# Interleaving GpSimd's weight loads with the scaling of v, ten more idle matmuls, and one group of scores behind the first MLP columns

## The chip, the core and the metric

The kernel runs on one core of one Trainium2 chip. The metric is the device time of one execution in microseconds (us). Before the change it is 312.73 us, the median of three runs (312.11 to 313.31). Five engines work side by side: TensorE (PE) multiplies matrices into PSUM banks; VectorE (DVE) and ScalarE (ACT) move PSUM results to SBUF and do elementwise work; GpSimd (POOL) works from SBUF to SBUF; SyncE (SP) only issues transfers. SP, ACT and POOL each have a DMA queue of their own, called q1, q10 and q0 in the profile.

## What is computed

The first half is a retention layer over 8 batches, 8 heads, 576 positions and a head width of 64. The second half is an MLP over the 4608 tokens that result.

```python
scores = scale * q @ k.T                       # per batch and head
gamma = 1.0 - 2.0 ** (-5.0 - arange(H))
Dmat = where(rel >= 0, gamma ** rel, 0.0)      # rel = row - column
x = ((scores * Dmat) @ v)                      # -> [4608 tokens, 512]
h = x @ w_in                                   # 512 -> 2048
out = (h * cos(h)) @ w_out                     # 2048 -> 512
```

## The kernel before, in words

**Retention.** A batch is cut into chunks of 128 positions (r = 0 to 3, and a short r = 4 with 64). The decay is split into a factor on q (table UP or UPN) and one on v (table WV), so that only a triangle mask is left for the scores. For each chunk PE does four things. `scores` multiplies k and q; its two results (one per head of a pair) are masked by two DVE operations of 128x512 (`mask`, L538). `sums_q` multiplies q by the state that the earlier chunks left in the SBUF tile `sb`, and `sums_v` adds the masked scores times v; the sum is copied into the tile `xt` (L595). `state` adds this chunk's k times v to the PSUM tile `st`, and two ACT copies (L616) take that to the next `sb`. `state` needs k of the chunk and the scaled v (tile `vb`) that POOL makes in `vmul` (L359). A scores group that is marked "later" has its second mask put behind the next MLP column group's multiplication on DVE.

**MLP.** The tokens go in 9 blocks of 512. `mlp1` makes one of 16 column groups (dt): four matmuls into a PSUM bank, the cosine on ACT (L644), the product on DVE (L647) into the tile `gt`. `mlp2` makes 128 rows of output from four parts of four matmuls each. There are four PSUM banks (`mm`) that `bank()` hands out in turn, so a column group has to wait until DVE has emptied the bank that was handed out four groups earlier. Block 1 is begun with the first 320 of its 512 tokens (SP1), since its last tokens belong to batch 2.

**Weights.** w_in comes in four pieces: columns for dt 0-1, 2-3, 4-7 and 8-15 (`WI`, L26). The first is loaded by SP as float32 into the space of q (`w_in_first`, L320) and turned to bf16 by one DVE operation of 128x1024 (`w_in_cast`, L330). The other three are loaded by POOL (`w_in_load`, L338), which converts on the way; so are the four pieces of w_out (L345).

**Order.** Everything is written out by hand in `emit` (L714 to L863); each engine does its instructions in that order and waits on semaphores. SP issues batch 0's k and q, v of chunks 0 to 3, the first piece of w_in (after POOL's casts of q have freed the space), and v of chunk 4. POOL casts k and q, scales v of chunk 0, issues w_in pieces 1 and 2, scales v of chunks 1 to 3, issues piece 3 and then w_out (L732 to L742). PE transposes k and q (`turn0`, `back0`), makes batch 0's scores (`scores0`, one group of 8 matmuls for each pair of heads, both results masked on DVE), then states and sums for chunks 1 and 2 (L765 to L770), then block 0's columns. DVE gets `w_in_cast` (L763) after the last masks and before the copies of the sums of chunks 1 and 2. `spin(n, bank)` (L498) issues n matmuls of 128x512 on a tile of zeros; nobody reads the result. In front of block 1 stand `turn_k(1, 2)` (a transposition of k, copied by ACT at L415), `rest(1, 1)` (sums and state of chunk 1), `scores(1, 2)` and one idle matmul (L816 to L819).

Of the kernel before, what the change touches and what calls it, by code (L numbers as in the profile page):

```python
# [48 lines left out]
class Sched:  # L49
# [36 lines left out]
    def done(self, eng, inst, reads, writes):  # L86
        self.count[eng] += 1
        inst.then_inc(self.sem[eng], 1)
        clock = {s: v for s, (v, _) in self.seen[eng].items()}
        t = Tok(eng, eng, self.count[eng], clock)  # L90
        self.record(t, reads, writes)
        return t
# [32 lines left out]
class _Kernel:  # L125
# [588 lines left out]
    def emit(self):  # L714
# [15 lines left out]
        self.w_in_first()  # L730
        self.load("v", 0, NCH - 1)
        self.vmul("pool", 0, 0)  # L732
        self.w_in_load(1)
        self.w_in_load(2)
        for r in range(1, NCH - 1):
            self.vmul("pool", 0, r)
        self.w_in_load(3)
        wo = []
        for i in range(NWO):
            wo.append(self.w_out_load(i))  # L740
# [3 lines left out]
        po, st = (self.PO, self.bPO), (self.ST, self.bST)  # L744
        mm, sc = list(zip(self.MM, self.bMM)), list(zip(self.SC, self.bSC))
        sc = [sc, [po, mm[3]]]
        self.spin(7, st)
        for c in range(NP):
            self.turn0("k", c, mm[0], "act" if c else "dve")
            if c:  # L750
                self.back0(c - 1, st)
            else:
                self.spin(1, mm[3])
            self.turn0("q", c, mm[1 + c % 2], "dve")
            if c < 2:
                self.spin(1, mm[3])
            if c:
                self.scores0(c - 1, sc[(c - 1) % 2])
        self.back0(3, st)
        self.state(0, 0)()  # L760
        self.scores0(3, sc[1])
        outs = [mm[0], mm[1], mm[2], sc[0][0]]
        self.w_in_cast()  # L763
        self.spin(3, mm[0])
        for r in (1, 2):  # L765
            done = self.state(0, r)
            self.sums_q(0, r, outs[r])
            done()
            for i in range(0 if r == 1 else 2, r + 1):
                self.sums_v(0, i, outs[i], "dve" if i else "act")()  # L770
        self.n_mm = 3
        self.vmul("pool", 0, NCH - 1)
        for r in range(NCH):
# [41 lines left out]
        self.flush()  # L815
        self.turn_k(1, 2, self.bank())  # L816
        self.rest(1, 1, self.bank())
        self.scores(1, 2)
        self.spin(1)  # L819

        for dt in range(16):
            self.mlp1(1, dt, 0, SP1)
            if dt in (7, 13):
                self.scores(1, 2 + dt // 6, True)
            if dt in (3, 9):
                self.turn_k(1, 3 + dt // 6)
            if dt in (5, 11):
                self.rest(1, 2 + dt // 6)
# [63 lines left out]
```

## Time and profile before

| what | number |
|---|---|
| median of three runs | 312.73 us (312.11 to 313.31) |
| the profiled execution | 312.78 us, of which the span of the profile is 311.0 us |
| PE busy | 303.1 us, 97% of the span |
| DVE, ACT, POOL busy | 178.3, 161.2, 106.5 us |
| mean granted TensorE clock | 0.995 |
| PE busy from 0 to 15.5 us, from 15.5 to 24 us | 11.38 of 15.5, 7.92 of 8.5 us |
| PE busy from 80 us to the end | 228.5 of 231 us |

All times in the views are counted from the start of the span. A row of a timeline gives the start, the length, the engine, the line, the operation, the tiles (output <- inputs), the number of instructions merged into it and, in brackets, the engine's idle time just before with what ended it. A row of the chain of work gives start, length, engine and line; the chain is followed back from the last instruction, so whatever stands in it set the end. In tables of stretches the columns are the stretch, its length, the busy time of each engine with its count of instructions, the granted PE clock (1.00 is full), the busy share of the DMA engines, and GB/s.

### The profile page before, as it was taken

What the parts mean: (1) busy time and instruction counts of PE and PEld (TensorE: products, weight loads), DVE (VectorE), ACT (ScalarE), POOL (GpSimd) and SP (SyncE); (2) the same over time, 40 slices, a digit from 0 to 9 for tenths busy, and PEclk for the clock granted to TensorE, in tenths of its full rate; (3) what the DMA queues carried; (4) which work ended last, traced back from release to release, by engine and by line L of the source; (5) the groups of instructions that cost most, each with busy time, mean ns of one, the idle gap of its engine ahead of it and who ended that gap; (6) DMA issues with size and microseconds to landing.
All of it is one profiled execution on the core that took longest, in us unless ns stands there. A gap on an engine that the chain in (4) does not pass through costs nothing.

```text
span 311.0 us, 6450 instructions
## 1 busy us (share of the span) xinstructions
PE 303.1 (97%) x2538; PEld 159.0 (51%) x2538; DVE 178.3 (57%) x318; ACT 161.2 (52%) x288; POOL 106.5 (34%) x129
## 2 busy tenths in 40 slices
PE   6799999999999999999999999999999999999996
PEld 3574455666644455445544554455445554444444
DVE  5857644887548842785368554855487448405800
ACT  8658407875447433753277236723573347316711
POOL 4881046645565636354646554510000000000000
PEclk9979999999999999999999999999999999999999
DMA  7999999999999999999999998950101010120022
GB/s 230 252 198 208 208 216 247 250 229 182 249 222 179 233 208 228 181 229 200 251 195 221 237 222 195 191 136 34 36 0 70 34 36 0 40 98 0 1 76 95
DMA packets 138319, 49.12 MB, mean 158 GB/s; under 512 B 127921, under 2 KB 132273, under 8 KB 138289
## 3 DMA queue, kind: packets, MB, share of 16 engines
q1 hardware_dynamic: 128880, 34.88, 61.8%
q10 hardware_dynamic: 5184, 9.31, 8.9%
q0 software_dynamic: 4224, 4.52, 8.7%
q8 instruction: 20, 0.33, 0.5%
q14 instruction: 11, 0.08, 0.1%
HBM read 36.70 MB, written 9.44 MB: 148 GB/s over the span
## 4 chain that ended last, share of the span: by engine, by line
PE 92%; SPq 3%; DMA 2%; ACT 1%; DVE 0%; issue 0%; ACTq 0%
PE mm L511 62%; PE mm L513 20%; PE po L511 5%; PE sc L511 3%; DMA qn<-in_moe_w_in_dram 2%; SPq L288 2%; SPq L296 1%; PE st L511 1%; ACT osb L681 1%; PE po L513 0%; ACT kqt L415 0%; DVE win L330 0%; DVE xt L595 0%; ACT xt L595 0%; ACT sb L616 0%
## 5 line engine op out<-in xcount | busy, mean ns | idle before, releaser
L647 DVE TENSOR_TENSOR gt<-mm,cb 128x512 bf16<-128x512 f32 (+3 forms) x164 | 101.6, 626 | 61.2 <-ACT cb L644 58.6
L511 PE MATMUL mm<-xt,win 128*128 128x512 bf16 (+3 forms) x492 | 119.1, 353 | 0.5 <-DVE xt L595 0.4
L644 ACT ACTIVATE cb<-mm,c_pih 128x512 bf16<-128x512 f32 (+3 forms) x164 | 102.8, 636 | 31.1 <-PE mm L513 30.7
L511 PE MATMUL mm<-wout,gt 128*128 128x512 bf16 (+1 forms) x450 | 117.4, 373 | 0.0
L511 PEld LDWEIGHTS mm<-xt,win 128*128 128x128 bf16 x492 | 46.4, 98 | 48.8 <-DVE xt L595 1.0
L511 PEld LDWEIGHTS mm<-wout,gt 128*128 128x128 bf16 x450 | 41.0, 98 | 42.2 <-DVE gt L647 0.2
L513 PE MATMUL mm<-xt,win 128*128 128x512 bf16 (+3 forms) x164 | 57.9, 353 | 0.0
L513 PE MATMUL mm<-wout,gt 128*128 128x512 bf16 (+1 forms) x142 | 53.6, 378 | 0.0
L681 ACT ACTIVATE osb<-mm 128x512 f32<-128x512 f32 x35 | 20.9, 597 | 62.5 <-PE mm L513 62.5
L359 POOL TENSOR_TENSOR vb<-vn,wv 128x512 bf16<-128x512 f32 (+1 forms) x40 | 41.6, 1042 | 11.3 <-DMA vn<-in_v_dram 10.1
L595 DVE CAST xt<-po 128x512 bf16<-128x512 f32 (+1 forms) x34 | 21.3, 627 | 40.5 <-PE po L513 40.5
L370 POOL CAST kqb<-kn 128x512 bf16<-128x512 f32 (+1 forms) x35 | 21.3, 610 | 66.7 <-DMA kn<-in_k_dram 61.7
L616 ACT ACTIVATE sb<-st 64x256 bf16<-64x256 f32 x64 | 24.2, 377 | 35.7 <-PE st L513 34.7
L359 POOL TENSOR_TENSOR kqb<-qn,upn 128x512 bf16<-128x512 f32 (+1 forms) x30 | 31.3, 1042 | 14.5 <-DMA qn<-in_q_dram 13.6
L538 DVE TENSOR_TENSOR rt<-sc,mk 128x512 bf16<-128x512 f32 (+1 forms) x52 | 29.1, 597 | 6.5 <-PE sc L513 6.5
L513 PEld LDWEIGHTS mm<-xt,win 128*128 128x128 bf16 x164 | 16.0, 98 | 15.4
L513 PEld LDWEIGHTS mm<-wout,gt 128*128 128x128 bf16 x142 | 13.9, 98 | 16.5
L511 PE MATMUL po<-rt,vb 128*64 128x128 bf16 (+1 forms) x245 | 13.6, 220 | 0.0
L538 DVE TENSOR_TENSOR rt<-mm,mk 128x512 bf16<-128x512 f32 x20 | 12.8, 681 | 0.0
L511 PEld LDWEIGHTS po<-rt,vb 128*64 128x64 bf16 (+1 forms) x245 | 8.3, 108 | 5.5 <-DVE rt L538 2.1
L511 PE MATMUL sc<-kqt 64*128 64x128 bf16 (+1 forms) x196 | 10.3, 213 | 0.8 <-ACT kqt L415 0.8
L511 PE MATMUL st<-vb,kqb 128*64 128x64 bf16 x224 | 9.5, 198 | 1.5 <-POOL vb L359 0.8
(126 smaller groups left out, 166.5 us busy)
## 6 DMA issues: line engine op xcount, KB each, us to landing
out_dram<-osb ACTq DMA_DIRECT2D x35, 256.0 KB, 3.4
vn<-in_v_dram SPq DMA_DIRECT2D x32, 256.0 KB, 5.1
kn<-in_k_dram SPq DMA_DIRECT2D x28, 256.0 KB, 4.1
qn<-in_q_dram SPq DMA_DIRECT2D x24, 256.0 KB, 4.6
wout<-in_moe_w_out_dram POOLq DMA_DIRECT2D x4, 512.0 KB, 15.7
kn<-in_k_dram SPq DMA_DIRECT2D x4, 288.0 KB, 5.1
qn<-in_q_dram SPq DMA_DIRECT2D x4, 288.0 KB, 5.4
vn<-in_v_dram SPq DMA_DIRECT2D x8, 128.0 KB, 4.3
```

The lines of the kernel that those rows point to most:

```text
L288: return self.s.dma(eng, f"{x}n{r}", lambda e: e.dma_start(dst, src), writes=[self.bST32[x][r]], after=after)
L296: self.s.dma("sp", f"{x}0_{c}", lambda e: e.dma_start(dst, src), writes=[self.bN0[x][c]])
L359: self.s.op(eng, lambda e: e.tensor_tensor(bass.AP(t, o, [[pitch, ck], [D_, H_], [1, D_]]), self.staged(x, r, [[D_, H_], [1, D_]]), bass.A ...
L370: fn = (lambda e: e.activation(o, f, AF.Copy)) if eng == "act" else (lambda e: e.tensor_copy(o, f))
L511: self.nc.tensor.matmul(o, a, b, **kw)
L513: return s.done("pe", self.nc.tensor.matmul(o, a, b, **kw), reads, writes)
L538: self.s.op("dve", lambda e: e.tensor_tensor(bass.AP(self.RT[k][hp], 0, p3), bass.AP(sc[0], 0, p3), bass.AP(self.MK, 0, [[CH, ck], [0, NP] ...
L595: fn = (lambda e: e.activation(o, f, AF.Copy)) if eng == "act" else (lambda e: e.tensor_copy(o, f))
L616: s.op("act", lambda e: e.activation(bass.AP(self.SB[r % 3], 64 * hp * 512 + 64 * hp, [[512, 64], [128, NP], [1, D_]]), bass.AP(self.ST, 6 ...
L644: s.op("act", lambda e: e.activation(co, mo, AF.Sin, bias=self.C_PIH.ap(), scale=1.0), reads=[bm, self.bC], writes=[bcb])
L647: s.op("dve", lambda e: e.tensor_tensor(bass.AP(g, dt * TB + o, [[16 * TB, 128], [1, n]]), mo, co, ALU.mult), reads=[bm, bcb], writes=bg[o ...
L681: s.op("act", lambda e: e.activation(o.ap(), m.ap(), AF.Copy), reads=[bm], writes=[bo])
```

## The change

Three edits in `emit`, and no other.

```diff
         self.vmul("pool", 0, 0)
-        self.w_in_load(1)
-        self.w_in_load(2)
         for r in range(1, NCH - 1):
             self.vmul("pool", 0, r)
-        self.w_in_load(3)
+            self.w_in_load(r)
...
                 self.scores0(c - 1, sc[(c - 1) % 2])
+        self.spin(1, mm[0])
         self.back0(3, st)
+        self.spin(3, mm[0])
         self.state(0, 0)()
         self.scores0(3, sc[1])
         outs = [mm[0], mm[1], mm[2], sc[0][0]]
         self.w_in_cast()
-        self.spin(3, mm[0])
+        self.spin(2, mm[0])
         for r in (1, 2):
             done = self.state(0, r)
             self.sums_q(0, r, outs[r])
             done()
+            if r == 1:
+                self.spin(4, mm[0])
             for i in range(0 if r == 1 else 2, r + 1):
                 self.sums_v(0, i, outs[i], "dve" if i else "act")()
+        self.spin(2, po)
...
         self.turn_k(1, 2, self.bank())
         self.rest(1, 1, self.bank())
-        self.scores(1, 2)
-        self.spin(1)
+        self.spin(2)
 
         for dt in range(16):
             self.mlp1(1, dt, 0, SP1)
-            if dt in (7, 13):
+            if dt in (0, 7, 13):
                 self.scores(1, 2 + dt // 6, True)
```

First, POOL's order for batch 0 becomes v0, v1, w_in piece 1, v2, piece 2, v3, piece 3, where it was v0, pieces 1 and 2, v1, v2, v3, piece 3. Second, idle matmuls are added at four places of batch 0 and one is taken away at a fifth (1 + 3 - 1 + 4 + 2 = 9 more), and the single one in front of block 1 becomes two, which makes ten in all. Third, the scores of batch 1's chunk 2 go from the place in front of block 1 to the place behind its first column group, and their second mask goes behind the second column group's product on DVE.

## The prediction

> **What bounds the kernel now.** I read the page's chain of work first. It ends in a row of PE shares:
>
> ```profile
> PE 92%; SPq 3%; DMA 2%; ACT 1%; DVE 0%; issue 0%; ACTq 0%
> ```
>
> From 24 us on PE never rests for long, so a change there counts only if it takes work or a wait from PE. The 8% that are not PE lie at the start. So the second view is the chain in order of time, from 11 to 20 us (start, length, what):
>
> ```profile
> 11.47 6.26 DMA qn<-in_moe_w_in_dram
> 17.73 0.02 issue
> 17.75 0.93 DVE win L330
> 18.68 0.60 DVE xt L595
> 19.29 0.05 issue
> 19.33 0.50 PE mm L511 x3
> ```
>
> The reader is to see that the first column group of block 0 (PE at 19.33) waits for the copy of chunk 1's sums, that this copy stands on DVE behind the cast of w_in's first piece, and that the cast waits for that piece's transfer, landed at 17.73. From landing to PE it is 19.33 - 17.73 = 1.60 us. Neither PE nor POOL sets this: in PE's timeline the sums of chunk 1 were issued by 17.3.
>
> The third view is the table of stretches of 1 us (PE, PEld, DVE, ACT, POOL busy, clock, DMA share, GB/s):
>
> ```profile
> 14.00:15.00 1.00, 0.81 (x5) 0.19 (x3) 1.00 (x3) 0.52 (x2) 0.98 (x2) 1.00 0.84 193
> 15.00:16.00 1.00, 0.39 (x9) 0.35 (x10) 0.49 (x1) 0.00 (x0) 1.00 (x2) 0.72 1.03 229
> 16.00:17.00 1.00, 1.00 (x16) 0.80 (x16) 0.00 (x0) 0.76 (x2) 1.00 (x2) 0.50 1.09 214
> 17.00:18.00 1.00, 1.00 (x23) 0.94 (x20) 0.25 (x1) 0.77 (x2) 1.00 (x2) 0.50 1.33 185
> 18.00:19.00 1.00, 0.89 (x12) 0.45 (x9) 1.00 (x2) 0.59 (x2) 1.00 (x3) 0.58 1.24 196
> ```
>
> The granted clock falls to 0.50 for (0.28 + 0.50 + 0.50 + 0.42) x 2 = 3.4 us, from about 15.4 to 18.8, after a stretch in which PE was busy half the time. It is full again at 19.33, where PE comes onto the chain. So in this execution the half clock costs nothing, and idle matmuls that prevent it bring nothing by themselves.
>
> **Edit 1, POOL's order.** The queues' view shows what shares the DMA engines. From 14.75 to 15.25 only q1 (SP's) moves; from 15.25 to 17.5 q0 (POOL's) moves too (packets, MB, share):
>
> ```profile
> q1 hardware_dynamic: 188, 0.17, 115.0%
> ```
>
> ```profile
> q0 software_dynamic: 357, 0.18, 64.0%
> q1 hardware_dynamic: 279, 0.27, 50.0%
> ```
>
> q1 alone runs at 0.17 MB / 0.5 us, about 343 GB/s; beside q0 at 0.27 / 2.25, 120 GB/s. Piece 1, which POOL issues at 12.71, is what slows the first piece of w_in: q0's first packets come at 15.25 to 15.35, some 2.6 us after the issue began. In the new order v1 comes first. Its transfer was issued at 5.54 and takes 7.3, landing at 12.85; `vmul` takes 1.04; so POOL issues piece 1 at about 13.95 instead of 12.71, and q0's packets come at about 13.95 + 2.6 = 16.6. Until then the first piece has the engines alone. Its last 0.27 MB at 343 GB/s take 0.8 us, so it would end at 16.05 instead of 17.5 (gain 1.4, the one bound). But the engines are not in step: v3's transfer, just ahead on q1, still has a tail in the stretch from 14.75, and an engine that starts the piece at 15.1 with 32 packets of 1 KB, at the 50 ns that 343 GB/s over 16 engines gives, ends at 16.75. The other bound is no gain, if q0's packets come as early as before. I take landing at 16.9, a gain of **0.8**, near the late engine.
>
> Is PE ready then? State of chunk 1 waited for v1 (0.81 us idle, at 15.61). Now v1 is ready at 13.95, but `st` must be copied first (ACT L616, 13.76 + 0.79), so it starts at 14.6. State and `sums_q` take 0.5 at full clock (the same groups for chunk 3 at 20.22 to 21.0 show 0.12 to 0.3 each), four idle matmuls 4 x 0.216 = 0.86 (three 128x512 in 0.65), to 15.95; the masks that `sums_v` needs end at 15.49. Two `sums_v` at 0.28: 16.5. Chunk 2's state, `sums_q` and `sums_v`, 0.8, with v2 landed at 14.6 and scaled by 15.95: 17.3. Two idle ones: **17.75**. With the landing at 16.9, cast and copy end at 18.45, so PE still waits 0.7 and the idle matmuls hide in that wait. The single one and the three further up lie in PE's waits for ACT (0.17 at 12.32, 0.69 at 13.41). Edit 2 in batch 0 therefore costs 0; without the cover it would be 9 x 0.216 = 1.9 us.
>
> What is late next? Piece 3. It was issued at 17.41 and took 9.9, landing at 27.3; column group 8 needs it, and started at 27.44 where the pitch of 0.865 from 26.44 gives 27.31. Any gain ahead is lost if piece 3 doesn't come earlier. POOL issues it at 17.7, hardly later, but behind pieces 1 and 2 on q0. Beside q1 it moved 0.18 MB in 2.25 us, 80 GB/s; almost alone, from 17.25 to 17.75, 0.09 MB in 0.5 us, 180; quite alone, with the longer rows of piece 3 from 22 to 27, 209. Starting at 16.6 with little beside it (v4's 0.13 MB fit into the gap before q0 begins), piece 1 (0.26 MB) takes about 1.5 us at 180, piece 2 (0.52) 2.5 and piece 3 (1.05) 5.0 at 209: 25.6, and landing, some 0.3 later, at about 26, or 26.4 with v4 in the way. Then group 8 comes at 26.5, and 0.1 of its small wait goes as well. Gain at that point **0.9** (bounds: 1.5 earlier, 1.25 later, the latter if q0 runs no faster than before and only starts later). Piece 2 is needed at 23.84 and landed at 22.8; it moves the same way. From 24 us PE is busy 35.24 of 36, so a shift is kept.
>
> Behind POOL's queue nothing else changes: v3 ends at 17.7 as before, w_out is issued at 18.5, and mlp2 needs w_out at 34.3, after 29.8.
>
> The Trainium skill, "DMA: Bandwidth & Descriptors", section "Issuing engines are not separate DMA queues", says that transfers from all issuing engines run on the same 16 DMA engines and interleave. By that alone an order that only moves bytes wins no total time, and piece 3 would land as before; the two rates above say that a mix of the two queues moves less than each alone.
>
> **Edit 3, the scores.** PE's timeline in front of block 1:
>
> ```profile
> 52.95 0.29 PE L511 MATMUL st<-vb,kqb 128*64 128x64 bf16 x7
> 53.04 0.20 PE L513 MATMUL st<-vb,kqb 128*64 128x64 bf16 x1
> 53.99 0.39 PE L511 MATMUL sc<-kqt 64*128 64x128 bf16 x7 [0.76 <-ACT kqt L415]
> 54.17 0.22 PE L513 MATMUL sc<-kqt 64*128 64x128 bf16 x1
> 54.32 0.39 PE L513 MATMUL mm<-zero,ident 128*128 128x512 bf16 x1
> 54.55 0.57 PE L511 MATMUL mm<-xt,win 128*128 128x320 bf16 x3
> ```
>
> The wait of 0.76 looks like the gain. But group 0 needs the copy of chunk 1's sums, DVE 53.15 + 0.69 = 53.84, so PE begins it at 53.9, not at 53.2; the two idle matmuls (0.43) lie in that wait. Scores behind it cost 0.425 (the same group at 60.09 lengthens the pitch of 0.545 to 0.97). Group 1: 53.9 + 0.545 + 0.425 = 54.87 instead of 55.09, gain 0.22. Then DVE is late. Before, both masks lay ahead of the first product; now between products. How DVE fares is seen where a later group has it so already:
>
> ```profile
> 61.28 0.68 DVE L538 TENSOR_TENSOR rt<-sc,mk 128x512 bf16<-128x512 f32 x1
> 61.88 0.48 DVE L647 TENSOR_TENSOR gt<-mm,cb 128x320 bf16<-128x320 f32 x1
> 62.27 0.68 DVE L538 TENSOR_TENSOR rt<-sc,mk 128x512 bf16<-128x512 f32 x1
> 62.87 0.48 DVE L647 TENSOR_TENSOR gt<-mm,cb 128x320 bf16<-128x320 f32 x1
> ```
>
> Mask to product 0.6, product to mask 0.4. Product 0 starts 1.37 after group 0 (54.55 to 55.92), at 55.27; mask 55.67, product 1 56.27, mask 56.67, product 2 57.27, done 57.75. Group 5 takes product 2's bank (six groups on, since `turn_k` at dt 3 takes one). PE would be there at 57.35 and waits until 57.8; before, group 5 was at 57.57. So the edit costs **0.23** (bounds: -0.22 without the wait, +0.45 with the products at 0.53).
>
> **Sum.** -0.9 + 0.2 = -0.7 us. The profiled execution took 312.78 (span 311.0 and 1.78 around it), 0.05 above the median. So span 310.3, time **312.1**.
>
> **Rivals.**
> - *More on both edits* (0.24): the first piece at the rate of q1 alone, landing at 16.35, 1.4; piece 3's wait 0.1; no wait on DVE, 0.2: 312.78 - 1.7 = 311.1. For it: 343 GB/s is measured. Against: the late engine, the mask rows. The clock would add to it: the half-clock stretch ended only 0.5 us ahead of PE's place in the chain, and an execution in which it lies later pays up to half of 3.4 us, which the idle matmuls would save; the three runs differ by 1.2. The Trainium skill, "TensorE: Matmul & The Clock Gate", Part 1, says that the gate looks at windows of about 3.4 us that run freely, not from a kernel's start. The length agrees; no run here shows the phase.
> - *The transfer is hidden anyway* (0.18): piece 3 lands at 27.3 as before, since the same bytes go through. Nothing is left of the front's gain, and edit 3 costs 0.23: 313.0.
> - *Slower* (0.18): q0 starts 1.25 us later and runs no faster, as it moved without a pause from 15.35 to 27. Piece 3 then lands at 28.55, and group 8 waits 1.25 longer than before: with edit 3, 314.3. It decides once piece 3 lands after 27.3. For it: q0 is at 96 to 123% share from 17.5 on. Against: its rate beside q1 was 80 GB/s at first.
>
> **How the numbers follow.** The forecast has 0.40. 0.5% of 312.7, about what a measurement of this kernel can tell from no change, is 1.6 us: 311.2 and 314.3 are the edges. Faster by more: the first rival, with its late clock, 0.24. Slower by more: most of the last, 0.13. Within: 0.63. The range goes from just under the first rival, 310.9, to 313.9, which leaves out the worst of the last.
>
> **What would show it.** Landing of the first piece at 16.9 and PE's group 0 at 18.5; q0's first packets near 16.6; piece 3 landed by 26.4, group 8 at 26.5; clock 1.00 from 15 to 19; group 1 of block 1 earlier by 0.2 against `turn_k`, and a DVE wait of about 0.45 ahead of group 5. I'm wrong if q0 starts as before, if piece 3 stays at 27.3, or if PE reaches 18.5 still busy with idle matmuls.

## The result, and the profile after

The changed kernel takes 314.32 us (median of 22 runs, 312.89 to 315.47) against 312.89 us before (22 runs). The ratio is 1.0041, with a 95% interval of 1.0023 to 1.0058: 1.3 us slower, with nothing of the forecast gain of 0.7. The profiled execution took 314.93 us with a span of 313.2, which is 2.2 us above the profiled execution of before, so its profile shows more loss than the median does.

The page's chain of work for the changed kernel, by engine:

```profile
PE 89%; DMA 6%; POOL 2%; SPq 1%; DVE 0%; ACT 0%; issue 0%; DVEq 0%
```

PE's share has gone down from 92% and DMA's up from 2%: a transfer stands in the chain for longer than before. Which one is told by the chain in order of time, from 11 to 30 us (start, length, what):

```profile
13.68 0.86 POOL win L338
14.55 0.02 issue
14.56 1.06 POOL vb L359
15.62 0.73 POOL win L338
16.35 0.02 issue
16.37 0.99 POOL vb L359
17.36 11.87 DMA win<-in_moe_w_in_dram
29.23 0.14 issue
29.37 0.81 PE mm L511 x3
```

The chain no longer runs through w_in's first piece. It runs through POOL, in its new order, to the issue of piece 3 at 17.36; piece 3 takes 11.87 us instead of 9.9 and lands at 29.23; column group 8 of block 0 starts at 29.37. Before, that group started at 27.44:

```profile
27.44 0.81 PE L511 MATMUL mm<-xt,win 128*128 128x512 bf16 x3
```

PE's timeline in the changed kernel shows the waits on the way (in brackets the idle time, and what ended it):

```profile
18.85 0.50 PE L511 MATMUL mm<-xt,win 128*128 128x256 bf16 x3 [1.02 <-DVE xt L595]
...
24.39 0.81 PE L511 MATMUL mm<-xt,win 128*128 128x512 bf16 x3 [0.88 <-DMA win<-in_moe_w_in_dram]
...
29.37 0.81 PE L511 MATMUL mm<-xt,win 128*128 128x512 bf16 x3 [1.36 <-DMA win<-in_moe_w_in_dram]
```

Group 0 does come earlier, 18.85 instead of 19.33. Then group 4 waits 0.88 us for piece 2 and group 8 another 1.36 us for piece 3. The front's gain of 0.48 is given back and 1.93 us are lost on top.

The clock did what the added matmuls were to do. In the table of stretches (PE, PEld, DVE, ACT, POOL busy, clock, DMA share, GB/s) it is full where it was half before:

```profile
15.00:16.00 1.00, 1.00 (x12) 0.34 (x11) 0.30 (x1) 0.54 (x2) 1.00 (x2) 1.00 0.97 271
16.00:17.00 1.00, 1.00 (x32) 0.85 (x30) 0.00 (x0) 0.69 (x2) 0.98 (x2) 1.00 1.02 133
17.00:18.00 1.00, 0.83 (x10) 0.24 (x8) 0.50 (x1) 0.55 (x2) 1.00 (x2) 1.00 1.27 178
18.00:19.00 1.00, 0.15 (x2) 0.14 (x3) 1.00 (x3) 0.00 (x0) 1.00 (x2) 1.00 1.14 126
```

The last column is the surprise: the DMA engines move 126 to 178 GB/s from 16 to 19 us, where it was 185 to 214 before. The third edit is seen at block 1. First PE's row of group 5 before, then PE and DVE in the changed kernel:

```profile
57.57 0.57 PE L511 MATMUL mm<-xt,win 128*128 128x320 bf16 x3
```

```profile
54.87 0.29 PE L511 MATMUL st<-vb,kqb 128*64 128x64 bf16 x7
...
55.83 0.58 PE L511 MATMUL mm<-xt,win 128*128 128x320 bf16 x3
...
59.75 0.58 PE L511 MATMUL mm<-xt,win 128*128 128x320 bf16 x3 [0.28 <-DVE gt L647]
```

```profile
57.21 0.49 DVE L647 TENSOR_TENSOR gt<-mm,cb 128x320 bf16<-128x320 f32 x1 [1.44 <-ACT cb L644]
57.62 0.68 DVE L538 TENSOR_TENSOR rt<-sc,mk 128x512 bf16<-128x512 f32 x1
58.22 0.48 DVE L647 TENSOR_TENSOR gt<-mm,cb 128x320 bf16<-128x320 f32 x1
58.62 0.68 DVE L538 TENSOR_TENSOR rt<-sc,mk 128x512 bf16<-128x512 f32 x1
59.22 1.46 DVE L647 TENSOR_TENSOR gt<-mm,cb 128x320 bf16<-128x320 f32 x3
```

From the state of chunk 1 to group 5 it is 59.75 - 54.87 = 4.88 us; before it was 57.57 - 52.95 = 4.62. The masks between the products hold group 5 up, and the edit costs 0.26 us in this execution. So 1.93 + 0.26 = 2.19 us is the whole difference of the two spans.

### The profile page after: what moved, and what is told of

Same layout as the page of the kernel before. It is cut to its first block, busy times and chain, and to the rows that moved or that the text cites. A ratio compares the mean times of both kernels' runs of the same rounds, so it can differ in the third digit from the quotient of the medians.

```text
span 313.2 us, 6470 instructions
## 1 busy us (share of the span) xinstructions
PE 305.3 (97%) x2548; PEld 158.8 (51%) x2548; DVE 177.7 (57%) x318; ACT 161.0 (51%) x288; POOL 106.9 (34%) x129
## 4 chain that ended last, share of the span: by engine, by line
PE 89%; DMA 6%; POOL 2%; SPq 1%; DVE 0%; ACT 0%; issue 0%; DVEq 0%
PE mm L511 61%; PE mm L513 19%; PE po L511 5%; DMA win<-in_moe_w_in_dram 4%; PE sc L511 3%; DMA vn<-in_v_dram 2%; POOL vb L359 1%; PE st L511 1%; SPq L296 1%; POOL win L338 1%; PE po L513 0%; DVE xt L595 0%; ACT cb L644 0%; DVE gt L647 0%; ACT osb L700 0%
## 5 line engine op out<-in xcount | busy, mean ns | idle before, releaser
L681 ACT ACTIVATE osb<-mm 128x512 f32<-128x512 f32 x35 | 20.9, 597 | 62.6 <-PE mm L513 62.6
L359 POOL TENSOR_TENSOR kqb<-qn,upn 128x512 bf16<-128x512 f32 (+1 forms) x30 | 31.2, 1041 | 15.7 <-DMA qn<-in_q_dram 15.5
L538 DVE TENSOR_TENSOR rt<-sc,mk 128x512 bf16<-128x512 f32 (+1 forms) x52 | 29.2, 596 | 5.9 <-PE sc L513 5.9
L513 PEld LDWEIGHTS mm<-xt,win 128*128 128x128 bf16 x164 | 16.0, 98 | 15.4
L513 PEld LDWEIGHTS mm<-wout,gt 128*128 128x128 bf16 x142 | 13.9, 98 | 16.6
L511 PE MATMUL po<-rt,vb 128*64 128x128 bf16 (+1 forms) x245 | 13.6, 220 | 0.0
L538 DVE TENSOR_TENSOR rt<-mm,mk 128x512 bf16<-128x512 f32 x20 | 12.8, 680 | 0.0
L511 PEld LDWEIGHTS po<-kqt,sb 128*128 128x128 bf16 x84 | 6.8, 98 | 6.3
```

The source lines that it names most:

```text
L359: self.s.op(eng, lambda e: e.tensor_tensor(bass.AP(t, o, [[pitch, ck], [D_, H_], [1, D_]]), self.staged(x, r, [[D_, H_], [1, D_]]), bass.A ...
L511: self.nc.tensor.matmul(o, a, b, **kw)
L513: return s.done("pe", self.nc.tensor.matmul(o, a, b, **kw), reads, writes)
L538: self.s.op("dve", lambda e: e.tensor_tensor(bass.AP(self.RT[k][hp], 0, p3), bass.AP(sc[0], 0, p3), bass.AP(self.MK, 0, [[CH, ck], [0, NP] ...
L681: s.op("act", lambda e: e.activation(o.ap(), m.ap(), AF.Copy), reads=[bm], writes=[bo])
```

## The experiments

All ratios are against the kernel before, run beside on the same chip, with 95% intervals; each kernel ran 12 times. Times within a kernel come from its one profiled execution.

**One edit at a time.** The order alone, the idle matmuls of batch 0 alone, and the moved scores alone.

```diff
# e1_order
-        self.w_in_load(1)
-        self.w_in_load(2)
         for r in range(1, NCH - 1):
             self.vmul("pool", 0, r)
-        self.w_in_load(3)
+            self.w_in_load(r)
```

> The order on GpSimd alone (v1, piece 1, v2, piece 2, v3, piece 3), without the idle matmuls and with the scores in their old place. Theory Q (the queue of pieces 1 to 3 starts later and runs no faster, so pieces 2 and 3 land late): it has nearly the whole loss of the change, column groups 4 and 8 of block 0 wait for their pieces, group 8 starts 1 to 2 us after the 27.44 of before, and the kernel is 1.0 to 2.0 us slower. Theory M (the idle matmuls or the scores are what costs): within 0.5 us of before.

Measured: 313.69 us, 1.0024 (1.0006 to 1.0041). Group 0 starts at 17.9, 1.45 us earlier than before; group 8 at 28.95, 1.5 us later, when piece 3 has landed at 28.8. The order is slower by itself, by less than theory Q had said (0.75 us, not 1 to 2), and the loss is where Q put it.

```diff
# e2_idle: the nine spins of batch 0, for instance
+                self.spin(4, mm[0])
...
+        self.spin(2, po)
```

> The nine idle matmuls of batch 0 alone. Theory Q: they lie in waits of TensorE, so the time is that of before to within 0.4 us, and the granted clock stays at 1.00 from 15 to 19 us where v1 is still late. Theory M: 0.5 to 1.9 us slower (nine at 0.216 us on the path).

Measured: 313.02 us, 1.0002 (0.9985 to 1.0019), clock 1.00 in all 12 executions and in every stretch from 14 to 20 us. Theory M falls.

```diff
# e3_scores
-        self.scores(1, 2)
-        self.spin(1)
+        self.spin(2)
...
-            if dt in (7, 13):
+            if dt in (0, 7, 13):
```

> The scores of batch 1's chunk 2 behind block 1's first column group, and two idle matmuls in front, alone. From the rows: group 1 of block 1 0.2 us earlier against the state of chunk 1, group 5 0.25 us later, because VectorE has two masks between the products; 0.2 to 0.3 us slower. The rival, that the removed wait of 0.76 us is won: 0.5 to 0.8 us faster.

Measured: 313.05 us, 0.9999 (0.998 to 1.0019). A gain of 0.8 is excluded; a loss of 0.25 can't be told from none by time. By the profile group 5 comes 58.01 - 54.09 = 3.92 us after group 0, where it was 3.02 before (0.43 of the difference are the scores that stand between, the rest is DVE's lateness). From the state of chunk 1 to group 5 it is 4.88 us, as in the changed kernel.

**Why is piece 3 late?** In the changed kernel's trace some packets of pieces 2 and 3 take 0.3 to 2 us each, where the middle one takes 0.1 to 0.17. They come early in their piece. Four of piece 2's end together, at 20.64 to 20.75 us, and the longest of all, 1.97 us, ends at 21.52. The records name no DMA engine; that these packets are the first of their piece on their engine is read from their place in time. GpSimd is busy issuing w_out then (18.5 to 22.2 us), so the next kernel holds these issues back.

```diff
# e5_wout_later: the whole change, and
+            piece = self.w_in_load(r)
+            if r == 2:
+                two = piece
+        s.need("pool", two)
         wo = []
```

> The whole change, but GpSimd issues w_out, q of batch 1 and what follows only once piece 2 of w_in has landed (some 22 to 24 us instead of 18.5). Theory I (the long first packets of pieces 2 and 3 on some DMA engines, 1.2 to 2.0 us each and ending together near 20.7 and 22, come from GpSimd issuing w_out at that time): no such packets, piece 3 lands by 27 instead of 29.2, and the kernel is 1 to 2 us faster than the change. Theory L (the queue is only started later): piece 3 lands at 29 as with the change, and the time is the change's to within 0.4 us.

Measured: 314.22 us, 1.003 (1.001 to 1.0051). w_out was issued at 23.7; the long packets were still there (12 in piece 2, 15 in piece 3), piece 3 landed at 28.3, and the time is the change's to within what these runs tell. Theory I falls.

**Four orders without the other edits.** From here on two theories are set against each other. D says that a piece must be issued some time before the engines come to it, or they stand still; S says that only the start of the queue and a fixed rate count.

```diff
# e4_two_after_v1: v0 v1 p1 p2 v2 v3 p3
# e6_all_after_v0: v0 p1 p2 p3 v1 v2 v3
# e7_all_after_v1: v0 v1 p1 p2 p3 v2 v3
# e8_pieces_first: v0 p1 v1 p2 v2 p3 v3
```

> Order v0, v1, pieces 1 and 2, v2, v3, piece 3, without the other edits. Issues at about 13.8, 14.7 and 17.5 us. Theory D (the first packets of a piece come 2.6 us after its issue on the first DMA engines and 4 to 5 us after it on the last; an engine that has emptied the piece before stands still until then, and only issues that come too late for that cost): piece 2 is there when it is needed, no long first packets of it, piece 3 lands at 27.3 to 28, the time within 0.4 us of before. Theory S (the queue starts a microsecond later and moves its bytes at the old rate): piece 3 lands at 28.3 to 28.6, 0.7 to 1.2 us slower.

Measured: 313.03 us, 0.9998 (0.9975 to 1.0021). This speaks for D. (Its profiled execution took 322.71 us and isn't used for landings.)

> Order v0, pieces 1, 2 and 3, v1, v2, v3. Issues at 12.7, 13.6 and 14.4 us; v1 to v3 ready 0.8 us later than before. Theory D: no engine runs dry, piece 3 lands at 26.5 to 27 instead of 27.3, group 8 starts no later than 27.4; same or up to 0.6 us faster. Theory S: piece 3 lands as before, same time to within 0.3 us. A third, that the scaling of v is needed in time: state of chunk 1 at 16.4, sums late, group 0 later than 19.3, 0.5 us slower.

Measured: 312.97 us, 1.0 (0.9978 to 1.0022). The time fits D and S, and a loss of 0.5 us by late scaling of v isn't excluded by it (PE waited 1.5 us for v in the profile). The profiled execution fits neither: it was the longest of the twelve (314.41), and piece 3 landed at 29.0 although it was issued at 14.5 and had no long packet. Piece 1 itself landed late in it, at 20.4.

> Order v0, v1, pieces 1, 2 and 3, v2, v3. Issues at 13.8, 14.7 and 15.5 us: the queue starts 1.1 us later than before, but no piece is issued behind the scaling of v2 or v3. Theory D: few long first packets, piece 3 lands at 26.8 to 27.6, the time within 0.3 us of before or faster. Theory S: piece 3 lands at 28.3 to 28.6, 0.7 to 1.2 us slower.

Measured: 313.61 us, 1.0025 (0.9998 to 1.0051). Piece 3 landed at 26.7, as D said and S did not; but the median is slower, by what S had said. The clock is another reason for that: group 0 to 3 ran at half clock here (0.69, 0.50, 0.50, 0.60 from 18 to 22 us), after v2 had come late and PE had stood still from 16.0 to 17.1. The four executions with a full clock took 312.1 to 312.6, the four with 0.989 on average 314.8 to 315.1.

> Order v0, piece 1, v1, piece 2, v2, piece 3, v3: in turn, but each piece ahead of v. Issues at 12.7, 14.6 and 16.4 us; the queue starts as before. Theory D: engines that empty piece 1 by 17.3 to 18.4 wait for piece 2 until 18.5 to 19.5, piece 3 lands 0.3 to 1 us later than 27.3, 0.2 to 0.8 us slower. Theory S: piece 3 lands at 27.3, within 0.2 us of before.

Measured: 312.54 us, 1.0003 (0.9972 to 1.0034). Here D's expectation missed: no loss, and hardly a long packet, though the pieces take turns with v. So taking turns is not by itself what costs. This kernel shows the half clock on the chain, in the table of stretches:

```profile
18.00:19.00 1.00, 0.00 (x0) 0.00 (x0) 0.37 (x1) 0.00 (x0) 1.00 (x3) 1.00 1.28 248
19.00:20.00 1.00, 0.00 (x0) 0.00 (x0) 1.00 (x3) 0.00 (x0) 1.00 (x2) 0.58 1.22 200
20.00:21.00 1.00, 0.92 (x5) 0.67 (x6) 0.62 (x2) 0.00 (x0) 1.00 (x2) 0.50 1.28 214
21.00:22.00 1.00, 1.00 (x8) 0.75 (x7) 0.27 (x1) 0.47 (x1) 1.00 (x3) 0.50 1.11 207
```

PE is idle from 17.6 to 20.1, and block 0 begins at half speed; two executions of twelve were like this (316 us), nine with a full clock took 311.6 to 312.8.

**Orders with the idle matmuls in place.** So the remaining kernels keep the second and third edit, which holds the clock, and vary the order alone.

```diff
# f1_pieces_last: v0 v1 p1 v2 v3 p2 p3
# f2_after_v1:    v0 v1 p1 p2 p3 v2 v3
# f3_pieces_first: v0 p1 v1 p2 v2 p3 v3
# f4_old_order:   v0 p1 p2 v1 v2 v3 p3
```

> The whole change, but with order v0, v1, piece 1, v2, v3, pieces 2 and 3 on GpSimd: the queue starts as in the change, piece 2 is issued at about 16.6 instead of 15.5 us and piece 3 at about the same 17.4. Theory D (an engine that has emptied a piece stands still until the first packets of the next are there, 4 to 5 us after its issue at the latest): longer first packets of piece 2 than in the change, until 21 to 22; piece 2 lands at about 25, piece 3 at 29.5 to 30.5, and the kernel is 0.3 to 1.5 us slower than the change. Theory S (only the start of the queue and a fixed rate count): the change's time to within 0.3 us.

Measured: 314.71 us, 1.0048 (1.0027 to 1.0069). Piece 2 landed at 24.8 and piece 3 at 29.7, as D has it; the time can't be told from the change's.

> The whole change, but with order v0, v1, pieces 1, 2, 3, v2, v3: the queue starts as in the change, pieces 2 and 3 are issued at 14.5 and 15.3 us, v2 and v3 are scaled 1.5 us later. Theory D: no long first packets, piece 3 lands at 26.5 to 27.5, group 8 starts by 27.5; 1.2 to 2.3 us faster than the change, 0 to 0.8 us faster than the kernel before. Theory S: piece 3 lands at 28.5 to 29, the change's time to within 0.3 us.

Measured: 313.39 us, 1.0011 (0.9995 to 1.0028); piece 3 landed at 27.8. About 0.9 us faster than the change, a little less than the 1.2 to 2.3 that D had said, and not faster than before. POOL's queue started at 16.15, no earlier than the change's 15.65. So theory S falls: with a start as late, piece 3 lands 1.5 us earlier.

> The whole change, but with order v0, piece 1, v1, piece 2, v2, piece 3, v3: in turn, but each piece ahead of v. With the idle matmuls in place no execution has the half clock that two of twelve had without them (they were over 316 us). 311.8 to 312.8 us, 0.2 to 1 us faster than the kernel before. If instead turn-taking itself is what costs, it is within 0.4 us of the change (314.3).

Measured: 312.70 us, 1.0003 (0.9979 to 1.0028), eleven of twelve at full clock. As good as before, not better: the expected gain of 0.2 to 1 us isn't there, and one execution (315.01) had a half-clock stretch all the same. Piece 3 landed at 26.1 in the profiled execution (311.85).

> The idle matmuls and the moved scores together, with GpSimd's order of before. Both theories: within 0.4 us of the kernel before, granted clock 1.00 in every execution. If the two edits cost something together that neither showed alone, it is 0.5 to 1 us slower, and the order bears only the rest of the change's loss.

Measured: 312.83 us, 0.9991 (0.9975 to 1.0008), all at full clock. The second and third edit cost nothing together that these runs can tell (at most 0.08%), and the order bears the loss of the change.

**Piece 2, piece 3, or v between them?**

```diff
# g1_two_early:   v0 v1 p1 p2 v2 p3 v3
# g2_three_early: v0 v1 p1 v2 p2 p3 v3
# g3_other_work:  v0 v1 p1 X p2 p3 v2 v3    (X: a product like v's, read by nobody)
```

> The whole change, but with order v0, v1, pieces 1 and 2, v2, piece 3, v3: piece 2 issued at 14.5 us (1 us before the change), piece 3 at 16.3 (also 1 us before). Theory D with piece 2 as the late one: few long first packets, piece 3 lands at 27.5 to 28, about 313.4 us like the order with all three pieces behind v1. With piece 3 as the late one: it lands at 28 to 28.5, 313.8 to 314.2 us.

Measured: 313.39 us, 0.9997 (0.9977 to 1.0018); piece 3 landed at 26.8.

> The whole change, but with order v0, v1, piece 1, v2, pieces 2 and 3, v3: piece 2 issued at 15.5 us as in the change, piece 3 at 16.3. Piece 2 as the late one: long first packets of piece 2 as in the change, piece 3 lands at 28.5 to 29.2, within 0.4 us of the change (313.9 to 314.5). Piece 3 as the late one: 0.6 to 1 us faster than the change.

Measured: 314.45 us, 1.0036 (1.0014 to 1.0059); piece 3 landed at 28.8. The two kernels differ in one exchange, of v2 and piece 2, that is in 1.1 us of piece 2's issue; piece 3 is issued within 0.2 us of the same time. PE's timelines, first g1, then g2:

```profile
22.61 0.82 PE L511 MATMUL mm<-xt,win 128*128 128x512 bf16 x3
...
26.93 0.81 PE L511 MATMUL mm<-xt,win 128*128 128x512 bf16 x3 [0.70 <-DMA win<-in_moe_w_in_dram]
```

```profile
23.95 0.81 PE L511 MATMUL mm<-xt,win 128*128 128x512 bf16 x3 [1.03 <-DMA win<-in_moe_w_in_dram]
...
28.90 0.81 PE L511 MATMUL mm<-xt,win 128*128 128x512 bf16 x3 [1.34 <-DMA win<-in_moe_w_in_dram]
```

Both waits of the changed kernel, for piece 2 and for piece 3, are there in g2; in g1 the first is gone and the second halved. What the queues moved between 18 and 22 us (packets, MB, share of 16 engines), in the kernel before, in the changed one, and in g1:

```profile
q0 software_dynamic: 612, 0.65, 96.6%
q1 hardware_dynamic: 524, 0.13, 23.9%
```

```profile
q0 software_dynamic: 571, 0.52, 110.6%
```

```profile
q0 software_dynamic: 647, 0.81, 117.6%
```

In the changed kernel q0 has the engines to itself and yet moves less than it moved beside q1 before. The share says 111%: a packet of piece 2 that stands for 1.97 us counts as busy like one of 0.1, so the share doesn't show the loss; the bytes do.

> The whole change, but with order v0, v1, piece 1, a multiplication of the same shape whose result nobody reads, pieces 2 and 3, v2, v3: piece 2 issued at 15.5 us as in the change with no scaling of v needed in between; chunk 2's v is ready at 18.2. Theory D (only the time of the issue counts): long first packets of piece 2, piece 3 lands at 28.5 to 29.2, 313.9 to 315 us. If the scaling of v itself (its transfers or its readers) is what slows the queue: as with all three pieces behind v1, 313.4 us.

Measured: 314.57 us, 1.003 (1.0007 to 1.0053). The time is what D expects, but the profiled execution (314.19) shows another cause for its own: PE ran at half clock from 7.7 to 14.5 us, waits for no v, is busy with batch 0 until group 0 at 20.7, and piece 3, landed at 27.8, holds nobody up. Seven of the twelve had a full clock and took as long (314.1 to 315.0); v2, scaled by 18.65 only, may be what comes late there, but no trace shows one of them. So the time doesn't tell the two theories apart. The landing is against D: piece 2 was issued at 16.0, later than in g2, yet its longest early packet (1.10 us) was through by 19.15, and piece 3 landed 1.0 us earlier than in g2, where D had 28.5 to 29.2.

The kernel before and the kernels with the second and third edit, sorted by the issue of piece 2 (us; "long" is the time of packets of pieces 2 and 3 over 230 ns, beyond that of the middle packet, summed over the engines):

| kernel | issue of 2 | issue of 3 | long | piece 3 lands | median |
|---|---|---|---|---|---|
| f4_old_order | 13.3 | 17.1 | 0.1 | 26.9 | 312.83 |
| before | 13.6 | 17.4 | 2.5 | 27.3 | 312.89 |
| f3_pieces_first | 14.1 | 15.9 | 1.6 | 26.1 | 312.70 |
| g1_two_early | 14.4 | 16.2 | 3.5 | 26.8 | 313.39 |
| f2_after_v1 | 14.6 | 15.4 | 4.4 | 27.8 | 313.39 |
| e5_wout_later | 15.4 | 17.2 | 10.5 | 28.3 | 314.22 |
| g2_three_early | 15.5 | 16.3 | 6.7 | 28.8 | 314.45 |
| the change | 15.5 | 17.4 | 18.9 | 29.2 | 314.32 |
| g3_other_work | 16.0 | 16.8 | 6.4 | 27.8 | 314.57 |
| f1_pieces_last | 16.5 | 17.3 | 15.8 | 29.7 | 314.71 |

Up to 14.6 the medians lie within 0.7 us of each other; from 15.4 on they are 0.8 us or more above all of those (g3_other_work for a reason that its trace doesn't show). A landing is of one trace each, and varies: kernels with the same order on GpSimd differ by 0.9 to 1.3 us (the change 29.2 and e5_wout_later 28.3; e8_pieces_first 27.4 and f3_pieces_first 26.1).

Two things in these traces say which wait sets the landing. First, piece 3 lands 4.9 to 5.05 us after piece 2 in 14 of the 17 traces, in the changed kernel 4.98; so what is late is piece 2, and piece 3 follows. Second, in the steady stretch a packet starts 19 ns before the recorded end of the one before it on its engine, so that the packets of one engine can be strung together. In the changed kernel the string that ends last has 32 packets of piece 2, the first from 19.55 to 21.52, then the 32 of piece 3, without another wait, to 28.91. In g1 the last string is the same but for its first packet, from 17.81 to 18.96, and it ends at 26.49. One engine that waits so long for one packet makes the whole piece late.

## Why the prediction was wrong, step by step

**The bound was read rightly, and the next one was named.** Group 0 did wait for w_in's first piece. The prediction also said that a gain ahead is lost if piece 3 doesn't come earlier. That is what happened, and e1_order shows it most clearly: 1.45 us won at group 0, 1.5 us lost at group 8.

**The first piece.** A gain of 0.8 was forecast, to a landing at 16.9; it landed at 17.48 in the changed kernel and at 16.5 in e1_order. In the other kernels with v1 ahead of piece 1 it landed at 16.45 to 16.86 (g3_other_work: 17.38), so 16.9 was a fair figure. The size of the gain varies from execution to execution all the same: in e3_scores, with the old order, it landed at 16.3, in e2_idle at 18.8, and POOL's queue began at 14.8 in the one and at 14.3 in the other, 15.35 in the profile of before. (Of the working, 32 packets of 50 ns from 15.1 end at 16.7, not 16.75; nothing hangs on it.) The profile of before is one draw of this, and 0.5 us of front gain is less than its spread.

**The step that failed** is "Starting at 16.6 with little beside it, piece 1 takes about 1.5 us at 180, piece 2 2.5 and piece 3 5.0 at 209: 25.6". It lets piece 1 go alone and the three pieces follow each other without a gap. The issues to landing of the three pieces, before and in the changed kernel (pieces 1, 2 and 3 in this order):

```profile
DMA to landing us min/median/max: 6.0/9.2/9.9
```

```profile
DMA to landing us min/median/max: 6.5/8.7/11.9
```

POOL's queue began at 15.65, not at 16.6: 0.3 us later than before where 1.25 was forecast, as the piece was issued at 13.62 and its first packet came 2.0 us behind that, not 2.6. So it ran beside the first piece of w_in until 17.48, and landed at 20.14, 4.5 us after its first packet where the sum has 1.5; in no trace here did it take under 2.7. Piece 2 landed at 24.25, 4.1 us behind piece 1 where the sum has 2.5. Piece 3 landed 4.98 us behind piece 2, as the sum has it (5.0). With the 0.3 that the prediction gives from the last packet to the landing, 18.4, 20.9 and 25.9 became 20.1, 24.25 and 29.2: some 1.7 us by the term of piece 1, another 1.6 by that of piece 2, none by that of piece 3.

The gap that was left out is seen at piece 2. Before, it was issued at 13.6, 3.7 us before the first engine came to it at 17.3, and no packet of it stood for more than 0.64 us. In the new order it is issued at 15.5 and the engines come to it from 17.5 on; four packets stand until 20.7, 5.1 us after the issue, and one until 21.5, and the string of that one ends last. First packets of piece 3 stand too, until 22 or 23, but on strings that end earlier. From 17.5 to 21 q0 moved 0.49 MB alone, 139 GB/s and not 180 to 209. Piece 3 landed at 29.2 where 26 to 26.4 was forecast: 1.93 us lost at group 8 instead of 0.9 won, 2.8 us on these two terms.

**The slower rival** gave 314.3, the measured time, by "q0 starts 1.25 us later and runs no faster". Its landing of piece 3, 28.55, is near the 28.3 to 29.2 seen with this order. That is luck, for its reason is not the one: the queue began 0.3 us later than before, not 1.25, and f2_after_v1, which begins later still, lands piece 3 at 27.8 and takes 0.9 us less than the change. The time goes with the issue of piece 2: g1 against g2 is one exchange, and 1.06 us. That it is the time of the issue alone isn't shown, as the landing in g3_other_work says otherwise. The prediction had put this order's rate at "little beside it", and given the rival 0.18; with piece 3 landing at 27.30, when its reader was ready for it (27.31), the chain stood on two transfers at once, and that deserved more.

**The idle matmuls cost 0** as forecast (e2_idle, f4_old_order). The prediction also said that they bring nothing by themselves in the profiled execution, and that others might pay. They do: of the 134 executions of the kernel before that ran beside these experiments, 88 had a full clock (median 312.85), 43 one half-clock stretch (313.82) and 3 two. With the nine idle matmuls the clock was full in 116 of 118 executions, the changed kernel's among them, g3_other_work left out. There it was full in 7 of 12; in its profile the half clock runs from 7.7 to 14.5 us; the stretch that it follows lies ahead of the nine matmuls. The medians of e2_idle and f4_old_order don't show a gain from this beyond their intervals.

**The third edit** was right in mechanism and size: 0.23 forecast, 0.26 in the profile (and in that of e3_scores), by the wait on DVE ahead of group 5 that was named, 0.28 us long where 0.45 was forecast. By time it can't be told from zero.

**What stays open.** Why the first packets of a piece come 2 us after the issue on one engine and 5 to 6 on another isn't shown; that they wait on the descriptors is argued from their place and their common end only. How much of it is the time of the issue alone was to be shown by g3_other_work, which failed to: its time has another cause, and its landing fits the other theory, that the scaling of v between the issues slows the queue. One trace doesn't decide that. Why piece 1 took 4.5 us here and 2.7 to 5.0 elsewhere isn't shown either. And e6_all_after_v0 had one execution in which piece 3 was late with an early issue.

No order that was tried beats the kernel before beyond its interval. The best, f4_old_order and f3_pieces_first, are equal to it.

## What to carry to other kernels

Before you move a queue's work back to help another transfer, look at how long each of its transfers stood in the queue before the engines reached it (3.7 us here, for piece 2): a later issue eats into that time. When two transfers each land just ahead of their reader, a gain at the first is no gain until the second moves too. The orders here that kept piece 2 issued ahead, with the scaling of v behind it, lost nothing that could be told.

## What the runs showed that was not expected

The first packet of w_in's piece 1, for which GpSimd's queue was empty, came 1.6 to 3.0 us after the start of its issue in the 17 traces. Of piece 2 in the changed kernel, the last early packet was through 6.0 us after the issue. The Trainium skill, "DMA: Bandwidth & Descriptors", section "Latency and other measured facts", gives about 1 us to the first byte for this path; in these traces it was longer in every case.

The share of the DMA engines was 111% at 131 GB/s (18 to 22 us in the changed kernel) and 118% at 202 GB/s (g1): the recorded time of a packet has its wait in it.

The clock of the kernel before was halved for 3.4 us, from 15.43, after 3.4 us in which PE was not idle but busy for 1.92 us, 56% of them. The Trainium skill, "TensorE: Matmul & The Clock Gate", Part 1, has the half clock follow an idle window of that length; here windows that were 43% (e8_pieces_first) to 58% busy (e7_all_after_v1) were followed by one. Not every such stretch was: in e6_all_after_v0 PE was busy for 36% of 3.4 us, from 12.8, and the clock stayed full. With the nine matmuls of 0.216 us no 3.4 us that began between 10 and 17 us held less than 66% (f4_old_order; 70% in the changed kernel), and the clock stayed full there.
